# Order, input tile and last stores of the prepass in a gated mix of two attentions

## The chip, the core and the metric

One core of one Trainium2 chip runs the whole kernel. The metric is device time of one execution, in microseconds (us). The kernel before took 1770.2 us (median of 3 runs, 1770.02 to 1771.49).

## What is computed

The input x has 2048 tokens of 640 values, in bfloat16. The output is `g * a + (1 - g) * b`, with a gate g per token.

- `b` is local attention: 32 heads of width 20, where each token sees 8 tokens at distance 0, 2, ... 14 behind it.
- `a` is attention with a recurrent memory: 64 segments of 32 tokens, 32 heads of width 192. In front of a segment's 32 tokens stand 8 memory rows, which are the first 8 output rows of the segment before. So the segments run one after the other.

```python
for s in range(n_seg):                       # 64 segments
    h = jnp.concatenate([mem, xs], axis=1)   # 8 memory rows + 32 tokens
    q, k, v = (einsum('btd,dhe->bhte', h, W) for W in (Wq, Wk, Wv))
    scores = jnp.where(mask, einsum('bhqe,bhke->bhqk', q, k) * scale, -1e9)
    o = einsum('bhqk,bhke->bhqe', softmax(scores), v)
    o = einsum('bhte,hed->btd', o, Wo)
    mem = o[:, :8, :]                        # memory of the next segment
    outs.append(o[:, 8:, :])
x = A_x
out = sigmoid(x @ gate_w) * a + (1 - sigmoid(x @ gate_w)) * b
```

(This is the reference cut and slightly condensed.)

## The kernel before

**Part B** (`part_b`, L88 to L336; 0 to 232 us) computes `b` and the gate. x is transposed block by block, 512 tokens each (`make_xT`, L158), into a tile xT. From xT GpSimd (POOL) copies each block's tokens for the later segments (L184, L185, stored to DRAM), and the last 8 tokens of every segment into a tile zx (L190), which SyncE (SP) stores to a DRAM tensor zT_dram (L191). In the last quarter (L319 to L322) zT_dram is loaded back as tile zT, whose columns go by segment and token (s i), and POOL copies it into zTi, whose columns go by token and segment (i s). A step of part B is one block and one group of four heads. `proj` (L218), `scores` (L232) and `values` (L254) follow each other from step to step; DVE multiplies the exponentials by a band mask (L251).

**Prepass** (`prepass`, L419 to L477; 232 to 389.4 us). The last 8 tokens of each segment (positions 24 to 31) do not depend on the memory, so their Q, K and V for all 64 segments are computed at once, with 512 columns. `project_qk` (L426) does a pair of head groups: 24 groups of five matmuls of 128x512 (L438), each evacuated from PSUM into one tile ZS; ScalarE (ACT) and DVE take turns (L75, L77). When the pair is done two DMAs store ZS (L444), 8 segments first and then 56, in pieces of 192 values (384 B). `project_v` (L446) does one of four V rounds: four tiles ZV, 15 matmuls each (L453), and two stores of 192 KB per tile (L460). The order is pair 0, V 0, pair 1, V 1, pair 2, V 2, pair 3, V 3. Pairs read zT, V rounds read zTi. All results go into a DRAM tensor zpk_dram, one row of 1152 values per segment and partition: 384 of V, then 384 of K and 384 of Q.

**Part A** (`part_a`; 390 to about 1705 us) runs the 64 segments. A segment projects Q and K of the other 32 rows in eight groups (`m_qk`, L568; evacuated by `c_qk`, L577), transposes them (`t_qk`, L585), computes scores (`s_a`, L615 and `s_b`, L624), V (`m_v`, L661), the weighted sum (`pv_half`) and the output projection (`o_group`, L725). It loads the prepass's rows of the segment: `load_z` (L543) brings Q and K into part of the tile ZQ, and `load_vz` (L547) brings V. The scores need `load_z`; in the first segment all of these loads come right behind the prepass. For PE, ACT and DVE the order inside the loop is written out by hand; outside of it the order follows the program and the scheduler's priorities. The first segment's score matmul starts at 403.21 us. Part Z then multiplies the 8 last tokens of all segments by Wo in one go.

**Weights.** They are cut into 80 slices of 384 KB. 14 are streamed anew for each segment (tile wst, five buffers). 66 stay in SBUF and are loaded in four lots, as memory becomes free: "early" (21, during part B), "late 0" (24, when part B ends), "late 1" (8, asked for inside pair 3, L431) and "late 2" (13, after the prepass, L914). The lots are filled from a list that is sorted by first use (L371). All slice loads are issued by SP, in order.

**Queues.** SP and ACT issue the DMAs. Eight semaphores serve all of them in turn; a DMA waits until the transfer that used its semaphore before has landed. ACT also evacuates PSUM, in the same instruction order, so what stands behind a waiting DMA issue waits as well.

Of the kernel before, what the change touches and what calls it, by code (L numbers as in the profile page):

```python
# [10 lines left out]
BF = mybir.dt.bfloat16  # L11
# [4 lines left out]
N_EARLY = 21  # L16
N_MID = 8
ZVB = 4
N_LAST = 13
# [7 lines left out]
class _K:  # L27

    def __init__(self, ctx, tc, A_x, A_mem0, A_Wq, A_Wk, A_Wv, A_Wo, seg_len, B_wqkv, B_wo, gate_w, out):
# [22 lines left out]
        self.zctx = ExitStack()  # L52
# [35 lines left out]
    def part_b(self):  # L88
# [6 lines left out]
        self.zT_dram = self.dram.tile([128, KC, S // 32, 8], BF, name="zT_dram")  # L95
# [5 lines left out]
        with ExitStack() as ctx:  # L101
# [56 lines left out]
            def make_xT(b):  # L158
# [30 lines left out]
                zx = blkp.tile([128, KC, 16, 8], BF, name="zx_blk")  # L189
                nc.gpsimd.tensor_copy(zx[:].rearrange("p c s i -> p s c i"), xv[:, :, :, 24:32])  # L190
                nc.sync.dma_start(self.zT_dram[:, :, 16 * b:16 * b + 16, :].rearrange("p c s i -> p c (s i)"),  # L191
                                  zx[:].rearrange("p c s i -> p c (s i)"))
# [97 lines left out]
            zp = self.zctx.enter_context(tc.tile_pool(name="pre_z", bufs=1, side="right"))  # L290
            self.zT = zp.tile([128, KC, S // 4], BF, name="zT")
            self.zTi = zp.tile([128, KC, S // 4], BF, name="zTi")
            sel_ones = wp.tile([128, 160], BF, name="sel_ones")
            steps = [(b, g) for b in range((S + BQ - 1) // BQ) for g in range(8)]
# [7 lines left out]
            for i, (b, g) in enumerate(steps):  # L302
# [11 lines left out]
                if (b, g) == (1, 4):  # L314
                    self.build_sel(self.const, sel_ones[:])
# [3 lines left out]
                if (b, g) == (S // 512 - 1, 2):  # L319
                    nc.sync.dma_start(self.zT[:], self.zT_dram[:].rearrange("p c s i -> p c (s i)"))  # L320
                    nc.gpsimd.tensor_copy(self.zTi[:].rearrange("p c (i s) -> p c i s", i=8),
                                          self.zT[:].rearrange("p c (s i) -> p c i s", i=8))  # L322
# [33 lines left out]
    def weights_setup(self):  # L356
# [14 lines left out]
        use = [g for p in range(4) for g in (("qqkk"[p], 2 * (p % 2)), ("qqkk"[p], 2 * (p % 2) + 1), ("v", p))]  # L371
# [47 lines left out]
    def prepass(self):  # L419
# [6 lines left out]
        def project_qk(p, pool):  # L426
            m, Rp = "qqkk"[p], p % 2
            ZS = pool.tile([128, nseg, 192], BF, name="ZS")
            sls = [[self.get_slice((m, 2 * Rp + r, kc)) for kc in range(KC)] for r in range(2)]
            if p == 3:  # L430
                self.load_late(1)  # L431
            for r in range(2):
# [514 lines left out]
```

## Time and profile before

| What | us |
|---|---|
| median of the runs (3) | 1770.2 |
| the profiled execution's own time | 1772.28 |
| its span in the profile | 1770.6 |
| part B | 0 to 232.0 |
| prepass, first to last matmul | 232.03 to 389.39 |
| first segment ends | 428.43 |
| second segment ends | 448.87 |
| store of 56 segments of ZS, issue to landing, at 337.41 | 13.45 |
| one slice of 384 KB, alone | 3.1 to 3.2 |
| one slice more, while several load | 0.97 |

The profile comes from one execution. A row of a timeline gives start, duration, engine and line, tiles, count, and in brackets how long the engine was idle before it and what ended that. A row of "windows" gives the length of the stretch, the busy time of PE in it with the number of instructions that it is made of, the clock granted to the TensorE (1.00 is full), the busy share of the 16 DMA engines and what they moved. Rows of "DMA queue" give packets, MB, and the time that the packets took as a share of the 16 engines' time. "q10" is ACT's queue, "q1" SP's.

### The profile page before, as it was taken

Reading aid. Unit: us, or ns where it says so; the run is one execution under the profiler, and the core shown is the slowest. Engines: PE = TensorE matmul, PEld = TensorE weight load, DVE = VectorE, ACT = ScalarE, POOL = GpSimd, SP = SyncE. Lnnn points to the kernel's source line nnn. Section 1 sums busy time; section 2 is a strip of 40 time slices with the busy share of each in tenths; the row PEclk is TensorE's granted clock in tenths of the full one; section 3 lists DMA queues with packets and bytes.
Section 4 is the critical chain, followed back from the end, with each engine's and each line's share of the span. In section 5 each row is a group of like instructions: output and inputs, shape, how many; then the busy total and the mean of one; then the engine's idle time right before and its main releaser. Section 6 shows DMA issues by size and latency. Waiting matters only on the chain.

```text
span 1770.6 us, 82392 instructions
## 1 busy us (share of the span) xinstructions
PE 1675.4 (95%) x36512; PEld 995.8 (56%) x36527; DVE 651.8 (37%) x2047; ACT 869.2 (49%) x2377; POOL 75.0 (4%) x151
## 2 busy tenths in 40 slices
PE   6888999987999999999999999999999999999989
PEld 3555544434565655556555555555555555555557
DVE  4565532322333333333333333333333333333330
ACT  3766632223555555555555555555555555555550
POOL 6011000000000000000000000000000000000000
PEclk9999999998999999999999999999999999999999
DMA  5951176579999999899999989989989999998991
GB/s 161 331 128 50 38 258 164 154 234 328 290 303 303 303 301 306 297 297 311 302 298 303 306 284 304 302 289 297 304 297 298 301 298 303 303 296 292 306 299 30
DMA packets 283480, 467.81 MB, mean 264 GB/s; under 512 B 97524, under 2 KB 158452, under 8 KB 283124
## 3 DMA queue, kind: packets, MB, share of 16 engines
q1 hardware_dynamic: 181400, 403.14, 68.9%
q10 hardware_dynamic: 101724, 59.41, 11.6%
q8 instruction: 285, 4.67, 1.1%
q14 instruction: 71, 0.58, 0.1%
HBM read 428.13 MB, written 42.20 MB: 266 GB/s over the span
## 4 chain that ended last, share of the span: by engine, by line
PE 83%; ACT 6%; DMA 6%; issue 3%; DVE 1%; ACTq 0%; SPq 0%; POOL 0%; DVEq 0%; POOLq 0%
PE ps_qk L568 25%; PE ps_v L661 13%; PE ps_wo L725 11%; PE ps_qkT L585 6%; PE ps_S L615 5%; PE ps_pre L438 5%; PE ps_oT L684 3%; PE ps_z L879 3%; PE ps_bqk L224 3%; ACT bP L247 2%; PE ps_pre L453 2%; ACT ZQ L806 2%; PE ps_bv L211 1%; PE ps_mem L735 1%; PE ps_S L624 1%
## 5 line engine op out<-in xcount | busy, mean ns | idle before, releaser
L577 ACT CAST KV<-ps_qk 128x384 bf16<-128x384 f32 x448 | 208.5, 480 | 333.0 <-PE ps_qk L568 185.0
L568 PEld LDWEIGHTS <-hT 128*32 128x32 bf16 x10240 | 247.7, 96 | 154.5 <-DVE hT L738 12.8
L568 PE MATMUL ps_qk<-wlate_k,hT 128*32 128x384 bf16 x4352 | 269.9, 329 | 1.2 <-issue 0.9
L592 DVE COPY ZQ<-ps_qkT 128x384 bf16<-128x384 bf16 x256 | 91.6, 358 | 390.0 <-PE ps_qkT L585 220.3
L568 PE MATMUL ps_qk<-wres_q,hT 128*32 128x384 bf16 x4096 | 227.4, 329 | 4.6 <-ACT ZV L75 3.8
L633 ACT ACTIVATE ZQ<-ps_S 32x224 bf16<-32x224 f32 x512 | 178.1, 348 | 44.3 <-PE ps_S L624 39.8
L725 PEld LDWEIGHTS <-KV 128*32 128x32 bf16 x6144 | 154.1, 96 | 67.7 <-issue 20.2
L661 PE MATMUL ps_v<-wlate_v,hT 128*32 128x384 bf16 x2816 | 160.6, 329 | 0.0
L568 PE MATMUL ps_qk<-wst,hT 128*32 128x384 bf16 x1792 | 153.9, 329 | 1.0 <-issue 1.0
L661 PEld LDWEIGHTS <-hT 128*32 128x32 bf16 x5120 | 113.4, 96 | 72.7 <-issue 10.0
L725 PE MATMUL ps_wo<-wlate_oa,KV 128*32 128x384 bf16 x2560 | 140.5, 327 | 2.9 <-issue 2.8
L615 PE MATMUL ps_S<-ZQ,KV 128*128 128x160 bf16 (+1 forms) x1024 | 136.9, 238 | 3.3 <-DMA ZQ<-zpk_dram 3.3
L585 PE MATMUL ps_qkT<-ident,KV 128*128 128x128 bf16 x1536 | 130.7, 221 | 0.4 <-issue 0.3
L725 PE MATMUL ps_wo<-wlate_ob,KV 128*32 128x256 bf16 x2688 | 123.6, 275 | 7.3 <-issue 7.3
L585 PEld LDWEIGHTS <-KV 128*128 128x128 bf16 x1536 | 89.4, 98 | 61.9 <-issue 40.9
L695 DVE CAST KV<-ps_oT 128x192 bf16<-128x192 f32 x256 | 79.4, 351 | 64.8 <-PE ps_oT L689 64.8
L615 PEld LDWEIGHTS <-KV 128*128 128x128 bf16 (+1 forms) x1024 | 59.1, 95 | 72.6 <-issue 45.3
L695 ACT CAST KV<-ps_oT 128x192 bf16<-128x192 f32 x256 | 69.6, 326 | 59.0 <-PE ps_oT L689 59.0
L544 POOL COPY KTz<-ZQ 128x384 bf16<-128x384 bf16 x64 | 32.6, 509 | 1492.1 <-DMA ZQ<-zpk_dram 850.6
L661 PE MATMUL ps_v<-wst,hT 128*32 128x384 bf16 x1024 | 87.1, 330 | 9.1 <-DMA wst<-in_A_Wv_dram 9.1
L738 DVE CAST hT<-ps_mem 128x24 bf16<-128x24 f32 x126 | 22.6, 179 | 197.4 <-PE ps_mem L735 197.4
L668 ACT CAST KV<-ps_v 128x384 bf16<-128x384 f32 x192 | 92.4, 481 | 3.1
(127 smaller groups left out, 2316.8 us busy)
## 6 DMA issues: line engine op xcount, KB each, us to landing
wst<-in_A_Wq_dram SPq DMA_DIRECT2D x260, 384.0 KB
wst<-in_A_Wv_dram SPq DMA_DIRECT2D x260, 384.0 KB
wst<-in_A_Wk_dram SPq DMA_DIRECT2D x195, 384.0 KB
wst<-wscr SPq DMA_DIRECT2D x192, 384.0 KB
ZQ<-zpk_dram ACTq DMA_DIRECT2D x64, 192.0 KB
zpk_dram<-ZS ACTq DMA_DIRECT2D x4, 2688.0 KB
wscr<-in_A_Wo_dram SPq DMA_DIRECT2D x20, 384.0 KB
wlate_k<-in_A_Wk_dram SPq DMA_DIRECT2D x17, 384.0 KB
```

The lines of the kernel that those rows point to most:

```text
L224: nc.tensor.matmul(ps[:, 0:nn], lhsT=wqk[n][:, kc, 4 * g:4 * g + 4, :].rearrange("p h d -> p (h d)"), rhs=xT[:, kc, o0:o0 + nn], start=(kc ...
L438: nc.tensor.matmul(ps[:], lhsT=sls[r][kc][:, c0:c0 + 128], rhs=zT[:, kc, :], start=(kc == 0), stop=(kc == KC - 1))
L568: nc.tensor.matmul(pq[32 * j:32 * j + 32, 0:384], lhsT=hT[:, kc, :], rhs=sl[:, 384 * j:384 * j + 384], start=(kc == 0), stop=(kc == KC - 1 ...
L577: cp(sts[i], pqs[i][:, 0:384])
L585: nc.tensor.transpose(pT[:, t, :, :, :].rearrange("p j b i -> p (j b i)"), st[:, 128 * t:128 * t + 128], self.ident[:])
L592: nc.vector.tensor_copy(q_blocks(R)[:, 1:5, :, :].rearrange("p b c i -> p c b i"), pT.rearrange("p t j b i -> p (t j) b i"))
L615: nc.tensor.matmul(grid(h, par)[:, :, 0:80].rearrange("p j (b r i) -> p j b r i", r=2, i=8)[:, :, :, r, :], lhsT=KT[k0:k1, 12 * r + c:12 * ...
L633: nc.scalar.activation(E[ps], pSs[h][ps, :, 112 * j:112 * j + 112], ACT.Exp, scale=scale_a)
L661: nc.tensor.matmul(pvs[R][32 * j:32 * j + 32, 0:384], lhsT=hT[:, kc, :], rhs=sl[:, 384 * j:384 * j + 384], start=(kc == 0), stop=(kc == KC ...
L668: cp(V[R], pvs[R][:, 0:384])
L695: cps[j % 2](oTxs[2 * h + j // 2][:, 6 * (j % 2):6 * (j % 2) + 6, :], pos[j][:, 0:240].rearrange("p (c q) -> p c q", q=40)[:, :, 8:40])
L725: nc.tensor.matmul(pso[part][32 * jj:32 * jj + 32, 0:n], lhsT=oTxs[2 * (R // 2) + j // 2][:, 6 * (j % 2) + 3 * (R % 2) + t, :], rhs=o_weig ...
```

## The change

- V rounds come first, all four; then pairs 0, 1, 2, 3. All of them read zTi, in the order (i s). The evacuation of a pair reads PSUM as (i s) and writes (s i).
- zT, zT_dram, the store, the load and the POOL copy of zTi go. POOL copies the last tokens of each block straight into zTi (after the xh store). zTi is a tile TZ that lives for the whole kernel; in part A its bytes serve as K and V (KV), the K of the prepass (KTz) and a part ZA of what was ZQ. The rest of ZQ becomes ZB.
- Pair 3 is evacuated into two half tiles ZS0 and ZS1, each stored by itself in pieces of 96 values (192 B), 8192 pieces each. Pairs 0 to 2 have one store each instead of two.
- Early is 23 slices in place of 21, late 0 is 27 in place of 24, late 2 is 8 in place of 13. The list is sorted V, Q, K.
- The small memsets of V tiles (L206) go from POOL to DVE, and the masks (`build_sel`) are built at another point of part B.

```diff
-N_EARLY = 21
+N_EARLY = 23
-N_LAST = 13
+N_LAST = 8
...
+        self.TZ = self.const.tile([128, self.KC * self.S // 4], BF, name="TZ")
+        self.zTi = self.TZ[:].rearrange("p (c x) -> p c x", c=self.KC)
...
-                zx = blkp.tile([128, KC, 16, 8], BF, name="zx_blk")
-                nc.gpsimd.tensor_copy(zx[:].rearrange("p c s i -> p s c i"), xv[:, :, :, 24:32])
-                nc.sync.dma_start(self.zT_dram[:, :, 16 * b:16 * b + 16, :].rearrange("p c s i -> p c (s i)"),
-                                  zx[:].rearrange("p c s i -> p c (s i)"))
+                with tc.issue_after(xh_store.ins):
+                    nc.gpsimd.tensor_copy(zTi[:, :, :, 16 * b:16 * b + 16],
+                                          xv[:, :, :, 24:32].rearrange("p s c i -> p c i s"))
+                    if b == 3:
+                        self.build_sel(self.const, sel_ones[:])
...
-                    nc.gpsimd.memset(V[:, 640:652], 0.0)
+                    nc.vector.memset(V[:, 640:652], 0.0)
...
-                if (b, g) == (S // 512 - 1, 2):
-                    nc.sync.dma_start(self.zT[:], self.zT_dram[:].rearrange("p c s i -> p c (s i)"))
-                    nc.gpsimd.tensor_copy(self.zTi[:].rearrange("p c (i s) -> p c i s", i=8),
-                                          self.zT[:].rearrange("p c (s i) -> p c i s", i=8))
...
-        use = [g for p in range(4) for g in (("qqkk"[p], 2 * (p % 2)), ("qqkk"[p], 2 * (p % 2) + 1), ("v", p))]
+        use = [(m, R) for m in "vqk" for R in range(4)]
...
-            ZS = pool.tile([128, nseg, 192], BF, name="ZS")
+            if p < 3:
+                ZS = pool.tile([128, nseg, 192], BF, name="ZS")
...
             for r in range(2):
+                if p == 3:
+                    ZS = pool.tile([128, nseg, 96], BF, name=f"ZS{r}")
...
-                            nc.tensor.matmul(ps[:], lhsT=sls[r][kc][:, c0:c0 + 128], rhs=zT[:, kc, :],
+                            nc.tensor.matmul(ps[:], lhsT=sls[r][kc][:, c0:c0 + 128], rhs=zTi[:, kc, :],
...
-                        zc = 96 * r + 8 * (4 * t + j)
-                        self.evac(ZS[:, :, zc:zc + 8], ps[:].rearrange("p (s i) -> p s i", i=8))
-            z0 = 768 + 192 * (1 - Rp) if m == "q" else 384 + 192 * Rp
-            for s0, s1 in ((0, 8), (8, nseg)):
-                nc.scalar.dma_start(self.zpk_dram[s0:s1, :, z0:z0 + 192].rearrange("s p f -> p s f"), ZS[:, s0:s1, :])
+                        zc = 96 * r * (p < 3) + 8 * (4 * t + j)
+                        self.evac(ZS[:, :, zc:zc + 8], ps[:].rearrange("p (i s) -> p s i", i=8))
+                if p == 3 or r == 1:
+                    f0, f1 = (z0 + 96 * r, z0 + 96 * r + 96) if p == 3 else (z0, z0 + 192)
+                    nc.scalar.dma_start(self.zpk_dram[:, :, f0:f1].rearrange("s p f -> p s f"), ZS[:])
...
-        with tc.tile_pool(name="pre_zv", bufs=ZVB, side="right", reuse_waits="tile") as zvp, \
-                tc.tile_pool(name="pre_zs1", bufs=1, side="right", reuse_waits="tile") as zs1:
-            zT, zTi = self.zT, self.zTi
-            with tc.tile_pool(name="pre_zs0", bufs=1, reuse_waits="tile") as zs0:
-                project_qk(0, zs0)
-                project_v(0)
-                project_qk(1, zs1)
-                project_v(1)
-                project_qk(2, zs0)
-            project_v(2)
-            project_qk(3, zs1)
-            project_v(3)
-        self.zctx.close()
+        zTi = self.zTi
+        with tc.tile_pool(name="pre_zv", bufs=ZVB, side="right", reuse_waits="tile") as zvp:
+            for R in range(4):
+                project_v(R)
+        with tc.tile_pool(name="pre_zs0", bufs=1, reuse_waits="tile") as zs0:
+            project_qk(0, zs0)
+            with tc.tile_pool(name="pre_zs1", bufs=1, side="right", reuse_waits="tile") as zs1:
+                project_qk(1, zs1)
+            project_qk(2, zs0)
+        with tc.tile_pool(name="pre_zs2", bufs=1, side="right", reuse_waits="tile") as zs2:
+            project_qk(3, zs2)
...
-            ZQ = pers.tile([128, 224 + 768 + 1152], BF, name="ZQ")
+            ZB = pers.tile([128, 1536 + 160], BF, name="ZB")
+            KV, ZA = self.TZ[:, 0:1536], self.TZ[:, 1920:2528]
...
-                nc.scalar.dma_start(ZQ[:, 608:1376], self.zpk_dram[s, :, 384:1152])
+                nc.scalar.dma_start(ZB[:, 0:768], self.zpk_dram[s, :, 384:1152])
...
-    k.load_late(2)
+    k.load_late(2, "right")
```

More of the change, by code (lines that the diff above doesn't have):

```diff
@@ L51, in __init__ @@
         self.hTp = ctx.enter_context(tc.tile_pool(name="hTp", bufs=2))
-        self.zctx = ExitStack()
+        self.TZ = self.const.tile([128, self.KC * self.S // 4], BF, name="TZ")
+        self.zTi = self.TZ[:].rearrange("p (c x) -> p c x", c=self.KC)
         self._evac_i = 0
@@ L94, in part_b @@
         self.bsc_dram = self.dram.tile([S, 640], BF, name="bsc_dram")
-        self.zT_dram = self.dram.tile([128, KC, S // 32, 8], BF, name="zT_dram")
         self.oz_dram = self.dram.tile([S // 32, 128, 384], BF, name="oz_dram")
@@ L289, in part_b @@
             nc.scalar.preload_act_table_set("natural_log_exp_and_others")
-            zp = self.zctx.enter_context(tc.tile_pool(name="pre_z", bufs=1, side="right"))
-            self.zT = zp.tile([128, KC, S // 4], BF, name="zT")
-            self.zTi = zp.tile([128, KC, S // 4], BF, name="zTi")
+            steps = [(b, g) for b in range((S + BQ - 1) // BQ) for g in range(8)]
+            zTi = self.zTi.rearrange("p c (i s) -> p c i s", i=8)
             sel_ones = wp.tile([128, 160], BF, name="sel_ones")
-            steps = [(b, g) for b in range((S + BQ - 1) // BQ) for g in range(8)]
             self.first_store = None
@@ L314, in part_b @@
                 if (b, g) == (1, 4):
-                    self.build_sel(self.const, sel_ones[:])
                     self.hT0 = self.load_seg(0)
@@ L431, in project_qk @@
                 self.load_late(1)
+            z0 = 768 + 192 * (1 - Rp) if m == "q" else 384 + 192 * Rp
             for r in range(2):
+                if p == 3:
+                    ZS = pool.tile([128, nseg, 96], BF, name=f"ZS{r}")
                 for j in range(4):
@@ L523, in part_a @@
             pers = ctx.enter_context(tc.tile_pool(name="a_pers", bufs=1, reuse_waits="tile"))
-            ZQ = pers.tile([128, 224 + 768 + 1152], BF, name="ZQ")
-            Vz = ZQ[:, 224:608]
-            QTa = ZQ[:, 992:2144].rearrange("p (b r c i) -> p b r c i", b=6, r=2, i=8)
-            Es = [ZQ[:, 608 * h:608 * h + 224].rearrange("p (a f) -> p a f", a=2) for h in range(2)]
-            zst = ZQ[:, 32:416]
+            ZB = pers.tile([128, 1536 + 160], BF, name="ZB")
+            KV, ZA = self.TZ[:, 0:1536], self.TZ[:, 1920:2528]
+            Vz = ZA[:, 224:608]
+            QTa = ZB[:, 384:1536].rearrange("p (b r c i) -> p b r c i", b=6, r=2, i=8)
+            Es = [z[:, 0:224].rearrange("p (a f) -> p a f", a=2) for z in (ZA, ZB)]
+            zst = ZA[:, 32:416]
             oTz = zst.rearrange("p (c q) -> p c q", q=8)
-            whi = ZQ[:, 1376:1376 + 640]
-            KV = pers.tile([128, 1536], BF, name="KV")
+            whi = ZB[:, 768:768 + 640]
             KT = KV[:, 0:768].rearrange("p (c k) -> p c k", k=32)
@@ L534, in part_a @@
             oTxs = [v.rearrange("p (c q) -> p c q", q=32) for v in V]
-            a4 = pers.tile([128, 160], BF, name="a4")
-            KTz = pers.tile([128, 12, 32], BF, name="KTz")
+            a4 = ZB[:, 1536:1696]
+            KTz = self.TZ[:, 1536:1920].rearrange("p (c k) -> p c k", k=32)
             psm = ctx.enter_context(tc.tile_pool(name="psm", bufs=2, space=bass.MemoryType.PSUM, reuse_waits="tile"))
@@ L542, in load_z @@
             def load_z(s):
-                nc.scalar.dma_start(ZQ[:, 608:1376], self.zpk_dram[s, :, 384:1152])
+                nc.scalar.dma_start(ZB[:, 0:768], self.zpk_dram[s, :, 384:1152])
                 nc.gpsimd.tensor_copy(KTz[:].rearrange("p c (R i) -> p c R i", i=8),
-                                      ZQ[:, 608:992].rearrange("p (R c i) -> p c R i", c=12, i=8))
+                                      ZB[:, 0:384].rearrange("p (R c i) -> p c R i", c=12, i=8))
             def load_vz(s):
```

## The prediction

> **What bounds the kernel.** I read the page first, then the engines' busy time in windows around the end of the prepass, then the waits and the timelines there. All times are on the profiled execution's axis.
>
> ```profile
> span 1770.6 us, 82392 instructions
> PE 1675.4 (95%) x36512; PEld 995.8 (56%) x36527; DVE 651.8 (37%) x2047; ACT 869.2 (49%) x2377; POOL 75.0 (4%) x151
> ```
>
> TensorE is the bound, and what it computes does not change, so only its idle time can move. The windows show where that is (columns: length, PE busy with instructions, granted clock, DMA share, GB/s).
>
> ```profile
> 385.00:390.00 5.00, 4.34 (x20) 1.00 1.03 263
> 390.00:393.20 3.20, 0.01 (x4) 1.00 1.00 284
> 393.20:398.00 4.80, 4.37 (x62) 0.64 0.92 274
> 400.90:403.20 2.30, 0.00 (x0) 1.00 1.02 389
> 403.20:409.50 6.30, 6.29 (x94) 0.73 1.01 382
> 409.50:416.90 7.40, 0.04 (x4) 0.82 1.03 406
> 428.43:448.87 20.44, 20.20 (x509) 1.00 0.92 300
> ```
>
> The last prepass matmul ends at 389.39 (call this instant X) and the first of 64 segments at 428.43: 39.04 us, against 20.44 for the second segment, whose PE is busy 20.20. The loop from the second segment on keeps its instructions, order and waits; nothing is to be had there. So 18.6 us of transition are in play, and three waits make most of them:
>
> ```profile
> PE ps_v L661 <- DMA wst<-in_A_Wv_dram: 7.4, 1, 7.4
> PE ps_qk L568 <- ACT ZV L75: 4.1, 2, 3.8
> PE ps_S L615 <- DMA ZQ<-zpk_dram: 2.3, 1, 2.3
> ```
>
> The timelines of ScalarE's and SyncE's queues tell why:
>
> ```profile
> 382.82 9.63 ACTq L460 DMA_DIRECT2D zpk_dram<-ZV  x4
> 392.55 1.56 ACT L75 CAST ZV<-ps_pre 128x512 bf16<-128x512 f32 x3 [9.22 <-DMA wst<-in_A_Wk_dram]
> 396.60 0.73 ACTq L543 DMA_DIRECT2D ZQ<-zpk_dram  x1
> 397.45 6.71 SPq L399 DMA_DIRECT2D wlate_oa<-wscr  x6
> 404.20 4.40 SPq L399 DMA_DIRECT2D wlate_ob<-wscr  x7
> 409.13 3.26 SPq L401 DMA_DIRECT2D wst<-in_A_Wv_dram  x4
> ```
>
> ScalarE issues stores and evacuates, in order. A store whose semaphore (eight, used in turn) still belongs to a transfer in flight stands, and the evacuations behind it stand too: 9.22 us idle, and the loop's first matmuls start 3.80 late. Later the streamed V slice is queued behind 13 slices: the 7.4.
>
> **Part B.** Removed: the round trip and this POOL copy, which the DVE multiply beside it pays for:
>
> ```profile
> 142.13 4.83 POOL L321 COPY zTi<-zT 128x2560 bf16<-128x2560 bf16 x1 [9.89 <-DMA zT<-zT_dram]
> 144.30 3.76 DVE L251 TENSOR_TENSOR bP<-bP,band 128x968 bf16<-128x968 bf16 x2 [1.88 <-ACT bP L247]
> ```
>
> Two L251 take 1.46 elsewhere (728 ns mean), so 2.3 us of DVE, of which PE waited 1.26 at 149.15 (for DVE bo): −1.3. Added: the four 0.72-us copies (L190) become strided copies into TZ; by L321's 1.89 ns an element 1.21 each, and DVE may stand for it; and 20 small memsets go to DVE, which is idle over half of this stage (0.11 each on POOL). +0.6, between 0 and +2.3. build_sel is only moved, and two more early slices lengthen a load queue that ends long before the prepass. **Part B −0.7**, between −1.3 and +1.
>
> **Prepass.** 720 matmuls at 0.2159 us are 155.4; it took 157.36 (232.03 to 389.39), of which 1.9 are waits. Reading PSUM as (i s) and writing strided costs nothing: both engines' evacuations of a pair (ACT 593, DVE 692 ns) lie under 2.16 us of matmul; without that cover each ns longer would count 72 times. V first gives 32 ZV stores while late slices still load (before: 231.37 to 257.2); stores and loads then wait for each other's semaphores. With a ZV store at 3 to 4 us and eight semaphores ScalarE falls little behind eight PSUM banks: I take **−0.9**, half the waits gone, between −1.9 and +4 (a stand of 9.22 us less five spare banks at 1.08 us of matmul each).
>
> **The transition.** Price of a packet first. Two windows in which one queue moves almost alone:
>
> ```profile
> q10 hardware_dynamic: 5474, 2.10, 99.3%
> q1 hardware_dynamic: 2370, 0.70, 96.8%
> ```
>
> The first (339 to 347, ZS store) is 384-B packets: 0.993 x 16 x 8 us / 5474 = 23.2 ns on an engine. The second (103 to 106) is 320- and 256-B packets, mean 295 B: 19.6 ns. The line through them gives 15.5 at 192 B; I take 16. Bounds: 23.2 (no cheaper than 384 B) and 7.6 (bytes alone, at a 3072-B packet's 121 ns). A half tile is 8192 packets, 512 on each engine: 8.2 us by 16 ns, and about 2 to land. The whole store takes 13.45 today (issued 337.41), so two halves cost 16.4 us of DMA where one full store costs 11.9.
>
> Order in the built program: SyncE issues late1's eight slices when p=2's store has landed, about X−11.5 (X−25.9, +0.6 evacuation, +13.9). ScalarE issues half 0 at X−11.2 (X−12.95, +1.7). They share the engines: 8.2 + 2 + eight slices at 0.97 (7.8) + three streamed slices (2.6) = 20.6, half 0 lands at **X+9.4**. Behind the last evacuation ScalarE has, in order: the Vz load, which takes half 0's semaphore and so stands until X+9.4; half 1's store (X+10); two c_qk; load_z, which needs half 1 landed; c_qk(3). So:
> - X+1.0: PE enters the loop; the 3.8-us gap shrinks to 1.0.
> - X+3.5: PE wants c_qk(0)'s bank and stands to X+10.4 (6.9).
> - Half 1: 8.2 + 2 + four slices of late2 released by half 0 (3.9): lands X+23.8. PE stands again for c_qk(3) and the scores.
> - load_z: 4.6 more with late2's next slices beside it (today 6.57; in the loop 4.8 to 7.3): first score matmul at X+28.4. Today X+13.8.
> - From the first scores a steady segment needs 14.5 (434.35 to 448.87), plus 1.7 for half clock after the wait, as at 403: end **X+44.6**. The streamed V slice, behind eight slices instead of 13, lands near X+32.7; wanted at X+34.7. The 7.4 goes.
>
> 44.6 − 39.04 = **+5.6**. What is late next after the V slice is half 1 and load_z. Each ns of packet price moves two times 0.512 us: at 23.2 ns +13.0, at 7.6 −3.0.
>
> [...]
>
> **Sum:** −0.7 − 0.9 + 5.6 = **+4.0**. The profiled execution took 1772.28 (span 1770.6) and would take 1776.3; the median of the runs shown is 1770.2, so 1774.2. 0.2% (3.5 us) is about what a measurement of this kernel can tell from no change.
>
> **Rivals.**
> 1. *The stores do land early.* If half 0 lands by X+1.4 (late1 loads behind it, not beside it), all that follows is 8 us earlier; what is left is the shorter last queue: X+36.6, −2.4; with −1.6 total −4.0, **1766.2**. It decides at X+5.4: half 0 landing sooner than that makes the kernel faster. For it: a 192-KB ZV store lands in 3 us when alone. Against: the queues alternate, and 9.6 us of slices are released within 1.5 us of half 0.
> 2. *Halves cost as much as wholes*: 23.2 ns a packet, total +11.4, **1781.6**. For it: 320 and 256 B are already only 15% under 384. [...]
> 3. *The V rounds stall* on semaphores, +4 in place of −0.9: total +8.9, **1779.1**. For it: the 9.22 row. Against: no ZS store lies ahead of V now.
> 4. *It cancels*: half 0 at X+5.4; late1 gives way by half, **1770.2**. The edit then merely moves the wait from L661 to L615.
>
> **Chances.** Forecast 0.45 (of which 0.15 ends under +3.5); rival 1 0.22, rival 2 0.15, rival 3 0.08, rival 4 0.10. Faster by over 0.2%: 0.22 (rival 1; its −4.0 is past −3.5). Within: 0.15 + 0.10 = 0.25. Slower: 0.30 + 0.15 + 0.08 = 0.53. The range goes from rival 1 with part B and prepass at their low ends (−2.4 − 1.3 − 1.9 = −5.6, 1764.6) to rival 2 (1781.6); it leaves out cheap packets under rival 1 and dear ones with stalls, under 2 in 10.
>
> **What would show it.** Right: ScalarE's Vz load issue standing 8 us after X; c_qk(0) after it; a 6-us PE gap before the third projection, a longer one before L615's first scores, none at L661; half stores landing 14 to 21 us after issue, their packets at 16 ns; first segment ending 44 to 45 us after X; no 3.2-us L251. Wrong: half 0 landed before X+5, PE idle over 2 us in the V rounds, or a segment after the first that differs from 20.4 us.

## The result and the profile after

The changed kernel took 1781.07 us (median of 4 runs, 1779.57 to 1784.05) against 1770.11 us for the kernel before (4 runs, 1769.2 to 1771.49): ratio 1.0063 [1.0046, 1.0081]. Measured again with more runs, the same pair gave 1772.88 (12 runs) against 1765.3 (35 runs): 1.0035 [1.0015, 1.0054]. So it is slower, by 6 to 11 us. The profiled execution took 1779.57.

The page of the changed kernel, the two lines that answer those of before:

```profile
span 1777.4 us, 82403 instructions
PE 1672.4 (94%) x36527; PEld 997.5 (56%) x36527; DVE 651.0 (37%) x2065; ACT 869.2 (49%) x2377; POOL 71.3 (4%) x132
```

PE is busy 3 us less and the span is 6.8 us longer: idle time was added. X, the end of the last prepass matmul, is 384.29 here. The windows behind it (length, PE busy, PEld, DVE, ACT, POOL, granted clock, DMA share, GB/s; the share adds up the times of packets and can pass 1):

```profile
384.29:386.84 2.55, 2.55 (x60) 1.44 (x60) 0.69 (x1) 0.00 (x0) 0.00 (x0) 1.00 1.57 170
386.84:396.41 9.57, 0.00 (x0) 0.00 (x0) 0.00 (x0) 0.53 (x2) 0.00 (x0) 0.74 0.85 181
396.41:401.05 4.64, 4.63 (x49) 2.13 (x49) 0.72 (x2) 0.81 (x2) 0.00 (x0) 0.50 0.95 314
401.05:410.12 9.07, 0.00 (x1) 0.00 (x1) 0.36 (x1) 0.53 (x2) 0.00 (x0) 0.50 0.85 195
412.96:429.85 16.89, 16.12 (x360) 9.21 (x360) 5.30 (x20) 8.11 (x26) 0.51 (x1) 0.83 0.89 293
429.85:449.60 19.75, 19.59 (x494) 12.06 (x494) 7.30 (x27) 10.59 (x32) 0.51 (x1) 1.00 0.94 309
```

PE enters the loop at once, where before it came 3.8 us late, and then stands twice, 9.57 and 9.07 us; behind the first the granted clock is 0.50, behind the second 0.50 (410.12 to 412.96) and then 0.83. The waits of PE in the first segment name who released it:

```profile
PE ps_qkT L581 <- ACT TZ L573: 18.6, 2, 9.6
PE ps_S L611 <- DMA ZB<-zpk_dram: 2.3, 1, 2.3
```

The wait for the streamed V slice (7.4 before) is gone, the one for load_z is as long as it was, and 18.6 us for ScalarE's evacuation of Q and K is new. ScalarE's timeline shows why it is late:

```profile
383.25 0.58 ACT L76 CAST ZS<-ps_pre 128x512 bf16<-128x512 f32 x1 [1.57 <-PE ps_pre L436]
394.97 0.35 ACTq L544 DMA_DIRECT2D TZ<-zpk_dram  x1
395.44 0.40 ACTq L442 DMA_DIRECT2D zpk_dram<-ZS  x1
395.88 0.86 ACT L573 CAST TZ<-ps_qk 128x384 bf16<-128x384 f32 x2 [12.05 <-issue]
409.15 0.34 ACTq L539 DMA_DIRECT2D ZB<-zpk_dram  x1
409.59 0.86 ACT L573 CAST TZ<-ps_qk 128x384 bf16<-128x384 f32 x2 [12.10 <-DMA zpk_dram<-ZS]
```

Between 383.83 and 394.97 it does nothing: the Vz load (L544, issued at 394.97) has the semaphore of half 0's store (L442, issued at 371.60) and stands until that lands, at X+10.6. Then half 1 goes out, two evacuations follow, and load_z (L539) stands until half 1 has landed, at X+24.8. What the stages add to the span:

| stage | before | after | difference | forecast |
|---|---|---|---|---|
| part B | 232.03 | 225.90 | −6.1 | −0.7 |
| prepass | 157.36 | 158.39 | +1.0 | −0.9 |
| X to the end of the first segment | 39.04 | 46.07 | +7.0 | +5.6 |
| segments 2 to 63 | 1259.9 | 1263.9 | +4.0 | 0 |
| the rest (segment 64 and behind it) | | | +0.9 | 0 |
| span | 1770.6 | 1777.4 | +6.8 | +4.0 |

### The profile page after: what moved, and what is told of

Same layout as the page of the kernel before. It is cut to its first block, busy times and chain, and to the rows that moved or that the text cites. A ratio compares the mean times of both kernels' runs of the same rounds, so it can differ in the third digit from the quotient of the medians.

```text
span 1777.4 us, 82403 instructions
## 1 busy us (share of the span) xinstructions
PE 1672.4 (94%) x36527; PEld 997.5 (56%) x36527; DVE 651.0 (37%) x2065; ACT 869.2 (49%) x2377; POOL 71.3 (4%) x132
## 4 chain that ended last, share of the span: by engine, by line
PE 84%; ACT 6%; DMA 5%; issue 3%; DVE 2%; ACTq 0%; DVEq 0%
PE ps_qk L564 25%; PE ps_v L657 13%; PE ps_wo L721 11%; PE ps_qkT L581 6%; PE ps_pre L436 5%; PE ps_S L611 5%; PE ps_oT L680 3%; PE ps_z L875 3%; PE ps_pre L451 3%; PE ps_bqk L225 3%; ACT bP L248 3%; DMA zpk_dram<-ZS 2%; ACT ZB L802 2%; PE ps_mem L731 1%; PE ps_S L620 1%
## 5 line engine op out<-in xcount | busy, mean ns | idle before, releaser
L573 ACT CAST TZ<-ps_qk 128x384 bf16<-128x384 f32 x448 | 208.1, 479 | 356.5 <-PE ps_qk L564 185.3
L657 PE MATMUL ps_v<-wres_v,hT 128*32 128x384 bf16 x4096 | 224.0, 328 | 0.0
L721 PEld LDWEIGHTS <-TZ 128*32 128x32 bf16 x6144 | 153.8, 96 | 72.7 <-issue 24.3
L581 PE MATMUL ps_qkT<-ident,TZ 128*128 128x128 bf16 x1536 | 131.0, 222 | 18.6 <-ACT TZ L573 18.6
L721 PE MATMUL ps_wo<-wlate_oa,TZ 128*32 128x384 bf16 x2560 | 140.2, 327 | 3.4 <-issue 3.4
L611 PE MATMUL ps_S<-ZB,TZ 128*128 128x160 bf16 (+1 forms) x1024 | 137.2, 238 | 3.1 <-DMA ZB<-zpk_dram 2.9
L721 PE MATMUL ps_wo<-wlate_ob,TZ 128*32 128x256 bf16 x2688 | 124.2, 275 | 8.5 <-issue 8.4
L564 PE MATMUL ps_qk<-wlate_q,hT 128*32 128x384 bf16 x2304 | 130.0, 329 | 1.3 <-issue 1.1
L564 PE MATMUL ps_qk<-wres_q,hT 128*32 128x384 bf16 x1792 | 109.2, 329 | 0.2
L629 ACT ACTIVATE ZB<-ps_S 32x224 bf16<-32x224 f32 x256 | 89.0, 348 | 41.4 <-PE ps_S L620 38.3
L611 PEld LDWEIGHTS <-TZ 128*128 128x128 bf16 (+1 forms) x1024 | 59.0, 95 | 71.8 <-issue 44.6
L734 DVE CAST hT<-ps_mem 128x24 bf16<-128x24 f32 x126 | 22.5, 179 | 201.3 <-PE ps_mem L731 201.3
L664 ACT CAST TZ<-ps_v 128x384 bf16<-128x384 f32 x192 | 92.3, 481 | 3.2
```

Source lines behind the costliest of these rows:

```text
L564: nc.tensor.matmul(pq[32 * j:32 * j + 32, 0:384], lhsT=hT[:, kc, :], rhs=sl[:, 384 * j:384 * j + 384], start=(kc == 0), stop=(kc == KC - 1 ...
L573: cp(sts[i], pqs[i][:, 0:384])
L581: nc.tensor.transpose(pT[:, t, :, :, :].rearrange("p j b i -> p (j b i)"), st[:, 128 * t:128 * t + 128], self.ident[:])
L611: nc.tensor.matmul(grid(h, par)[:, :, 0:80].rearrange("p j (b r i) -> p j b r i", r=2, i=8)[:, :, :, r, :], lhsT=KT[k0:k1, 12 * r + c:12 * ...
L629: nc.scalar.activation(E[ps], pSs[h][ps, :, 112 * j:112 * j + 112], ACT.Exp, scale=scale_a)
L657: nc.tensor.matmul(pvs[R][32 * j:32 * j + 32, 0:384], lhsT=hT[:, kc, :], rhs=sl[:, 384 * j:384 * j + 384], start=(kc == 0), stop=(kc == KC ...
```

## The experiments

The stage that the forecast priced came out nearly as priced; two others, that it had near nothing for, moved by 6.1 and 4.0 us with opposite signs. Two questions follow: are those two the change's doing, and what sets the length of the transition? For the second there are three theories. **T1**, the prediction's: ScalarE issues and evacuates in order, so a store that lands late holds everything behind it. **T2**: the 192-B packets are dear, for a reason of size or address. **T3**: from X to the end of the first segment the DMA engines are full, and the length is the transfer work that is left at X; the order of the queues only chooses which instruction waits.

To compare runs I use one mark: the start of the first matmul that picks the memory rows, 0.5 us ahead of the first segment's end. It is at X+38.54 before and X+45.56 after; the loop in the table is counted between such marks.

### The two kernels once more

Nothing is changed in either.

> The changed kernel again, unedited, for a second profile. Theory 1 (the extra time sits in the transition; the loop's +4.4 us in the first pair of profiles is chance in how late instruction fetches come): transition from the last prepass matmul to the first segment's end again 46 us, but the mean of the later segments back at 20.3 us, and a median near 1776. Rival (the loop itself became slower by the change): mean segment again 20.40 us or more, median again near 1781. Part B: if its -6.1 us came from half-clock stretches that happened to miss this run, it will differ by 2 to 5 us this time; if it came from the copies, it stays at 225.9 us.

> The kernel before once more, for a second profile. Theory 1 (part B and the loop vary from run to run by several us for reasons that have nothing to do with the change): part B differs from 232.0 by more than 1 us, or the mean segment from 20.32; the prepass (157.4) and the transition (first segment's end at +39.0) stay within 1 us. Rival (part B of the kernel before is always near 232 and the copies were worth 4 to 6 us): 232 again.

Kernel after: ratio 1.0035 [1.0015, 1.0054], the first scores at X+29.5, the mark at X+45.90, prepass 158.39 again, part B 228.5, loop 1257.6. Kernel before (a single run): 1766.61 us, mark X+40.60, part B 226.49 in place of 232.03, loop 1253.5 in place of 1259.9. So the transition repeats to 0.3 us in the changed kernel and to 2.1 in the one before (its V slice came later, a wait of 8.6 in place of 7.4), while part B and the loop move by 5.5 and 6.4 us between two executions of the *same* kernel. Part B moves with the clock. One window of it in the kernel before, in the first profile:

```profile
205.00:220.00 15.00, 14.44 (x220) 9.51 (x220) 7.60 (x21) 9.67 (x27) 0.00 (x0) 0.77 0.07 24
```

and in the changed kernel:

```profile
205.00:220.00 15.00, 14.79 (x237) 10.68 (x239) 7.47 (x25) 8.35 (x27) 0.00 (x0) 1.00 0.10 36
```

A granted clock of 0.77 for 15 us against 1.00; the second profile of before has 1.00 there as well, and all versions of the changed kernel end part B anywhere from 225.9 to 231.1. The loop's waits, changed kernel, 450 to 1690 us:

```profile
PE ps_wo L721 <- issue: 14.6, 22, 1.3
PE ps_oT L680 <- issue: 4.6, 8, 0.9
```

In a version with the same loop (pad_64 below):

```profile
PE ps_wo L721 <- issue: 6.4, 11, 1.5
PE ps_oT L680 <- issue: 4.0, 8, 1.1
```

"issue" means that PE waited for nothing that the profile shows. Added up, these waits go from 16.5 to 27.0 us in the 14 profiles of this study, and the loop from 1251.6 to 1263.9; the correlation is 0.94, with 1.1 us of loop for 1 us of wait. The two profiles of before have 23.5 and 21.0, the changed kernel 26.0 and 22.8. So the loop's +4.0 lies within what one kernel does by itself.

### ScalarE without the stand: vz_from_sync

The first Vz load goes to SP's queue, so that ScalarE no longer waits for half 0.

```diff
-            load_vz(0)
+            nc.sync.dma_start(Vz, self.zpk_dram[0, :, 0:384])
```

> The first segment's Vz load is issued by SyncE, so that on ScalarE nothing stands ahead of the second half's store. Theory 1 (ScalarE stands on the semaphore of the first half, and this is what delays the second half): the second half's store is issued about 1 us after the last prepass matmul instead of 11, c_qk follows at once, the 9.6-us gap of PE goes, the second half lands at about +17 instead of +24.8, the first scores come near +21 instead of +28.7; 6 to 8 us faster than the changed kernel. Rival (the engines are full anyway, so that an earlier issue only shares them): second half lands at +22 or later, and the gain is under 3 us.

Ratio 1.0027 [1.001, 1.0045]; first scores X+26.3, mark X+43.13: 2.4 us earlier only. The waits:

```profile
PE ps_qkT L581 <- ACT TZ L573: 16.3, 2, 12.7
PE ps_S L611 <- DMA ZB<-zpk_dram: 2.3, 1, 2.3
```

Half 1 is issued at X+0.8 in place of X+11.15, yet lands at X+22.5 in place of X+24.8: it takes 21.7 us, because it now runs beside the other half. So the first stand of ScalarE, which T1 blames, is worth 2.4 of the 7.0 us by itself.

### The address of the halves: row_1280 and pad_64

A row of zpk_dram is 2304 B long and half 0 starts 1152 B into it. row_1280 makes every row a multiple of 512 B and leaves the offsets. pad_64 has the same row length and shifts K and Q by 64 values (128 B).

```diff
-        self.zpk_dram = self.dram.tile([nseg, 128, 1152], BF, name="zpk_dram")
+        self.zpk_dram = self.dram.tile([nseg, 128, 1280], BF, name="zpk_dram")
...
-            z0 = 768 + 192 * (1 - Rp) if m == "q" else 384 + 192 * Rp
+            z0 = 832 + 192 * (1 - Rp) if m == "q" else 448 + 192 * Rp
...
-                nc.scalar.dma_start(ZB[:, 0:768], self.zpk_dram[s, :, 384:1152])
+                nc.scalar.dma_start(ZB[:, 0:768], self.zpk_dram[s, :, 448:1216])
```

(The first edit is row_1280; all three are pad_64.)

> The rows of zpk_dram are 1280 values instead of 1152, so that every row begins on a multiple of 512 B and the first half's 192 B (offset 1152) no longer cross such a line in every second row; they still cross a 256-B line. Theory 1 (a piece that crosses a 512-B line costs twice): the first half runs at 262 GB/s like the second instead of 146, 12.6 ns a piece instead of 21; it lands 4 to 5 us earlier, at about +6, and so does all that follows: 4 to 5 us faster than the changed kernel. The whole store of pair 1 (at 1536, crossing none) lands in under 12 us, pairs 0 and 2 stay at 13.7. Rival (256-B lines matter, or the row pitch, or which half it is): first half stays at 146 GB/s, no gain.

> Rows of zpk_dram of 1280 values, and K and Q begin 64 values later: the first half's 192 B now lie within one 256-B line (1280 to 1472), the second half's cross one (1472 to 1664). Theory 2 (a piece that crosses a 256-B line is dear, 512-B lines having been ruled out): the roles change; the first half runs at 262 GB/s, the second at 146 where it is alone, and the first half lands 4 to 5 us earlier than in the changed kernel (+6), the second one as much later after its issue. Rival (it is not the place in DRAM, but the tile ZS0 or the order): first half again at 146 GB/s, landing at +10.6.

row_1280: ratio 1.0029 [1.001, 1.0048], half 0 lands at X+10.1, mark X+43.96; nothing of the 512-B row shows in the packets (half 0 moves at 149 GB/s from 387 to 390, in the changed kernel at 146 from 386.4 to 388.4). pad_64 is the telling one, though its mark (X+46.32) is that of the changed kernel and its time (1769.54, a single run, against 1767.35) settles nothing: the two halves trade places. Half 0 lands at X+7.6 (X+10.6 without the shift), half 1 takes 17.8 us (13.7). The DMA view of the changed kernel while half 0 is nearly alone, 386.4 to 388.4:

```profile
DMA packets 1487, 0.29 MB, mean 146 GB/s; under 512 B 1485, under 2 KB 1485, under 8 KB 1487
```

and half 1 of the same kernel, 403 to 407:

```profile
DMA packets 5129, 1.05 MB, mean 263 GB/s; under 512 B 5105, under 2 KB 5105, under 8 KB 5129
```

In pad_64, half 1, 404.4 to 407.4:

```profile
DMA packets 2271, 0.44 MB, mean 145 GB/s; under 512 B 2271, under 2 KB 2271, under 8 KB 2271
```

2 us on 16 engines for 1487 packets is 21.5 ns each, and 4 us for 5129 is 12.5; with the shift half 1 pays 3 us for 2271, 21.1. Half 0's pieces reach from byte 1152 to 1344 of a row and cross a 256-B boundary (1280), half 1's from 1344 to 1536 do not; with the shift it is the other way round, and so are the prices. A crossing costs about 8.8 ns a packet, 4.5 us for a half store. T2 is right in this form, not in the 512-B form.

The two prices are some 70% apart. Pieces of 384 B show what goes with the price. Pair 0's begin 128 B behind a boundary and pair 2's on one, and both cost 23.5 ns (5452 and 5442 packets in 8 us, 306 to 314 and 362 to 370 in the changed kernel). In all these cases it is how many 256-B lines a piece touches: 21 to 24 ns for two, 12.5 for one.

### Half 0 ahead of the slices: late1_last

Rival 1 asked for a half 0 that lands by X+1.4, late1 loading behind it. Here late1's eight slices move to the lot that is asked for after the prepass.

```diff
-N_MID = 8
+N_MID = 0
...
-N_LAST = 8
+N_LAST = 16
```

> No slices are loaded beside the last pair (N_MID 0), all 16 come after the prepass (N_LAST 16). Theory 1 (eight slices beside the first half delay it): the first half lands about 10 us earlier, near +1 or before, ScalarE does not stand, the second half is issued near +1.5 and lands near +17 beside slices; the first scores near +22; then the streamed V slice, behind 16 slices, is late by several us as in the kernel before. Sum about 1773 to 1777. Rival (the first half is slow by itself, at 21 ns a piece 10.8 us): it lands at about 0 all the same, so the two differ in the stand of ScalarE only if slices matter; should it land later than +5 with no slices beside it, theory 1 is wrong.

Ratio 1.0041 [1.0023, 1.0059]. Half 0 landed at X+1.38, as rival 1 has it (and took 14.07 us with nothing beside it, as long as a whole pair's store); the first scores came at X+20.9, 7.7 us earlier. But the mark is at X+45.37, not 8 us earlier:

```profile
PE ps_qkT L581 <- ACT TZ L573: 13.0, 1, 13.0
PE ps_v L657 <- DMA wst<-in_A_Wv_dram: 7.2, 1, 7.2
```

The V slice is late again, behind 16 slices. Rival 1 got its condition and lost its gain, though not quite in its own form: here late1's eight slices lengthen the last queue, which rival 1 has short. It fits T3: the same transfers, in another order, the same end.

### The last pair in one tile: whole_last, split_segments

whole_last stores the last pair like the others, in 384-B pieces. split_segments does that too, but in two stores, 8 segments and then 56, as the kernel before did.

```diff
-            if p < 3:
+            if True:
...
-                if p == 3 or r == 1:
-                    f0, f1 = (z0 + 96 * r, z0 + 96 * r + 96) if p == 3 else (z0, z0 + 192)
-                    nc.scalar.dma_start(self.zpk_dram[:, :, f0:f1].rearrange("s p f -> p s f"), ZS[:])
+            for s0, s1 in ((0, 8), (8, nseg)) if p == 3 else ((0, nseg),):
+                nc.scalar.dma_start(self.zpk_dram[s0:s1, :, z0:z0 + 192].rearrange("s p f -> p s f"), ZS[:, s0:s1, :])
```

(This is split_segments; whole_last has one store of all segments there.)

> The last pair in one whole tile again, one store; all else of the change stays. Theory 1 (halves cost a stand, since a half takes the engines about as long as a whole, and the first one meets eight slices): nothing stands ahead of the store, issued near +1.2 after the last prepass matmul, alone on the engines; lands at +15, first scores near +19 (changed kernel +28.7), streamed V slice late by 1 to 2 us, first segment's end near +37 to +38 instead of +46: 7 to 9 us faster than the changed kernel, 1 to 3 faster than the kernel before. Rival (halves bring the store forward by 13 us of matmul, so without them the scores come later): scores after +28, slower than the changed kernel.

> Last pair in one tile, stored as in the kernel before: 8 segments first, then 56. The first segment's load then needs only the short store. Theory 1: short store issued near +1.2, landed near +5, first scores near +10; the wait then moves to the streamed V slice, which stands behind late 2, and late 2 behind the long store (lands near +16): V slice near +27, first segment's end near +38, no gain over the whole store. Rival (late 2 does not matter with 8 slices): end near +27.

whole_last: ratio 1.0003 [0.9981, 1.0025], mark X+41.30, that is 4.3 us earlier than with halves. Its one store lands at X+17.75, the waits are 13.8 (ScalarE), 3.5 (V slice) and 1.1 (load_z). split_segments: ratio 1.0019 [1.0002, 1.0036], mark X+41.37; the early short store gained nothing at the end. It landed at X+6.11 and load_z went out at X+6.13, but load_z took 10.69 us: it is on ScalarE's own queue behind the long store, which landed at X+16.45. Most of that, 7.98 us, is the issue itself, in which ScalarE does nothing else:

```profile
393.05 7.98 ACTq L536 DMA_DIRECT2D ZB<-zpk_dram  x1
```

### Two more orders: split_z_sync, late2_after_v

split_z_sync is split_segments with the first load_z on SP's queue. late2_after_v is that, and the last eight slices are asked for only behind the first segment's V slices.

```diff
-                nc.scalar.dma_start(ZB[:, 0:768], self.zpk_dram[s, :, 384:1152])
+                (nc.scalar if s else nc.sync).dma_start(ZB[:, 0:768], self.zpk_dram[s, :, 384:1152])
...
-            self.nc.sync.dma_start(v[:], src)
+            self.last_load = self.nc.sync.dma_start(v[:], src).ins
...
+                if s == 0:
+                    with tc.issue_after(self.last_load):
+                        self.load_late(2, "right")
...
-    k.load_late(2, "right")
```

(The first edit is split_z_sync; all of them are late2_after_v.)

> As split_segments, but the first segment's load of K and Q is issued by SyncE, so that it isn't behind the long store in ScalarE's queue. Theory 1 (in split_segments that load took 10.7 us because it lay in one queue with the long store): it now lands in 4 to 6 us, first scores near +11 instead of +18.9; the streamed V slice then is what is late, since late 2 stands ahead of it until the long store has landed (+16.5): a stall of 9 us or more at the V matmuls, first segment's end again near +41, no gain in sum. Rival (the engines, not the queue, made it slow): scores after +16.

> As split_z_sync, and late 2 is issued behind the first segment's four V slices. Theory 1 (the order of the last queue is what is left): scores near +11, no stall at V, then one of some 4 to 7 us at the output projection, whose streamed slice is behind late 2; first segment's end near +31 to +33, 13 us before the changed kernel and 6 to 8 before the kernel before: ratio to before 0.996. Rival (the stall only moves, to the output projection, whole): end after +38, ratio 1.000 or more.

split_z_sync: ratio 1.0021 [0.9996, 1.0047], first scores at X+11.74 (28.68 in the changed kernel, 13.82 before), mark X+42.14. Its waits:

```profile
PE ps_v L654 <- DMA wst<-in_A_Wv_dram: 12.9, 1, 12.9
PE ps_S L608 <- DMA ZB<-zpk_dram: 6.5, 1, 6.5
```

late2_after_v: ratio 0.9998 [0.9971, 1.0025], mark X+39.56:

```profile
PE ps_wo L718 <- DMA wst<-wscr: 10.1, 1, 10.1
PE ps_S L608 <- DMA ZB<-zpk_dram: 6.5, 1, 6.5
```

Scores 17 us earlier made the end 3 to 6 us earlier. The wait walks from Q and K (18.6) to the V slice (12.9) and on to the output projection's slice (10.1); each kernel cures the last one's symptom. That is T3's picture. One order was not run: all of these issue the long store of segments 8 to 63 within 2 us of X, and none holds it back until the first segment has what it needs. The last eight slices would have to wait with it, since they wait for that store here (SyncE's wait in late2_after_v: `SPq L393 <- DMA zpk_dram<-ZS: 5.8, 1, 5.8`).

### Less left at X: v_last, v_last_left

If T3 holds, it takes less transfer work behind X to shorten the transition. v_last runs the pairs first and the V rounds last (as the kernel before ends), all pairs whole, with the list sorted Q, K, V. The K and Q stores have landed 45 us before X; what is left at X are V's small stores and the eight slices.

```diff
-        use = [(m, R) for m in "vqk" for R in range(4)]
+        use = [(m, R) for m in "qkv" for R in range(4)]
...
-        with tc.tile_pool(name="pre_zv", bufs=ZVB, side="right", reuse_waits="tile") as zvp:
-            for R in range(4):
-                project_v(R)
...
         with tc.tile_pool(name="pre_zs2", bufs=1, side="right", reuse_waits="tile") as zs2:
             project_qk(3, zs2)
+        with tc.tile_pool(name="pre_zv", bufs=ZVB, side="right", reuse_waits="tile") as zvp:
+            for R in range(4):
+                project_v(R)
```

v_last_left only takes `side="right"` away from the pool pre_zv.

> The changed kernel with the last pair whole and the order turned: four pairs first, then the four V rounds; the slices' list is sorted Q, K, V. All else of the change stays (one x^T, shared bytes, 8 slices at the end). Theory 3 (what sets the first segment's end is the DMA work that is left behind the last prepass matmul: 42 us of engine time in the changed kernel, 37 in the one before, 38 with a whole tile, however it is ordered): here the stores of K and Q lie under V's matmuls, and behind the end there are only the last V stores, 8 slices and the segment's own; load_z is issued before the end, scores near +5, V slice late by 0 to 3 us, DMA work behind the end under 27 us, first segment's end at +20 to +25: 13 to 18 us faster than the kernel before, ratio 0.990 to 0.993. Rival (V stores and slices collide at the end as in the kernel before, whose V rounds were last too): ScalarE stands behind a store as there, first segment's end at +33 or later, ratio 0.996 or more.

> As v_last (pairs first, V rounds last, last pair whole), but the ring of ZV tiles lies on the other side of the memory, where only its second tile overlaps the last pair's ZS. Theory (the 6.83-us wait at the start of the V rounds in v_last is that tile waiting for the store of ZS, and the transition is set by the transfers behind X): the waiting evacuation comes 14 matmuls, 3.0 us, later, so the wait shrinks to 3 to 4 us; prepass 163 instead of 166.8; first segment's end stays at X+26 to X+29; span 3 to 4 us under that of v_last at an equal mean segment; ratio 0.995 to 0.998. Rival (the wait is for weights of V, or for semaphores): the prepass stays at 166 to 167 and the ratio at 0.999. A second rival, that the first segment's early end was a matter of one execution: it ends at X+38 or later.

The stretch from X to the first segment's end, in windows: the kernel before,

```profile
389.39:428.43 39.04, 24.87 (x488) 14.22 (x487) 7.86 (x27) 11.79 (x34) 0.51 (x1) 0.83 0.95 323
```

the changed kernel,

```profile
384.29:430.36 46.07, 24.32 (x489) 13.49 (x489) 7.61 (x26) 10.31 (x31) 0.51 (x1) 0.70 0.92 245
```

and v_last, to its mark:

```profile
393.90:420.82 26.92, 20.85 (x473) 12.44 (x473) 7.72 (x26) 10.53 (x32) 0.00 (x0) 0.94 0.96 333
```

The DMA share is 0.92 to 0.96 in all three, and the length is what differs: 39, 46, 27. But the share is an average. It passes 1 while small packets move, whose times overlap (1.57 from 384.29 to 386.84), and so it hides stretches in which the engines have next to nothing to move. The changed kernel has two (length, PE busy, granted clock, DMA share, GB/s):

```profile
393.00:396.40 3.40, 0.00 (x0) 0.50 0.14 21
407.20:410.60 3.40, 0.48 (x3) 0.50 0.22 26
```

Each lies at the end of a half store. Half 0's packets are nearly all through by X+8.7 and the last one by X+9.6; the landing is told at X+10.6; only then are the Vz load, half 1 and the next of late 2's slices issued, and the engines are full again from X+12.1. The kernel before has no such hole; its emptiest stretch, under which PE works, is this:

```profile
420.50:425.50 5.00, 4.99 (x174) 0.94 0.66 188
```

So I split the time from X to the mark in two, counting no quarter of a microsecond as more than full (an estimate from the packets' records, one profile each):

| kernel | X to mark | DMA share | engines empty | engines moving |
|---|---|---|---|---|
| before | 38.5 | 0.95 | 2.9 | 35.6 |
| before_again | 40.6 | 0.92 | 4.3 | 36.3 |
| after | 45.6 | 0.92 | 8.6 | 37.0 |
| same_again | 45.9 | 0.91 | 9.3 | 36.6 |
| vz_from_sync | 43.1 | 0.98 | 5.1 | 38.0 |
| row_1280 | 44.0 | 0.94 | 7.5 | 36.5 |
| pad_64 | 46.3 | 0.93 | 8.8 | 37.5 |
| late1_last | 45.4 | 0.91 | 6.2 | 39.2 |
| whole_last | 41.3 | 0.92 | 6.4 | 34.9 |
| split_segments | 41.4 | 0.94 | 5.6 | 35.8 |
| split_z_sync | 42.1 | 0.90 | 6.9 | 35.2 |
| late2_after_v | 39.6 | 0.95 | 4.9 | 34.7 |
| v_last | 26.9 | 0.96 | 1.5 | 25.4 |
| v_last_left | 28.2 | 0.93 | 2.7 | 25.5 |

(The 42, 37 and 38 us of the expectation of v_last are length times share, which counts the overlap twice.) Half of T3 stands: the time that the engines move is about 35 to 39 us in every kernel but the two of v_last's order, which leave less at X and have 25. The program sets it, not the length: SyncE's queue moves 2654 to 2702 packets of 3072 B up to the mark in every kernel with eight late slices, in 27 us or in 46, against 3301 and 3310 in the kernel before and 3689 in late1_last. The other half of T3, that the engines are full, is wrong for the changed kernel. Its engines move for about 1 us longer than those of the kernel before, with fewer bytes (245 x 46.07 against 323 x 39.04: 11.3 and 12.6 MB), and are empty for about 5 us longer, which is most of its longer transition. vz_from_sync, in which half 1 is queued before half 0 has landed, has only the second hole left (2.5 us at a share of 0.15), and whole_last has one of 3.5 us (0.12). So T1's chain, a landing that everything behind it waits for, is where the change lost most of its time, and T3's work is a floor that no order but v_last's took below 34.7 us.

v_last takes 11.6 us out of the transition and is still no faster: ratio 0.999 [0.9968, 1.0011]; v_last_left 0.9996 [0.9977, 1.0015]. The prepass gives it back. PE's waits in v_last's prepass:

```profile
PE ps_pre L449 <- ACT ZV L76: 6.8, 1, 6.8
PE ps_pre L434 <- DVE ZS L78: 2.3, 3, 0.8
```

ScalarE's wait behind the first is `ACT ZV L76 <- DMA zpk_dram<-ZS`, 15.3 us: the first ZV tile lies where the last pair's ZS lay, whose store of 13.9 us must land first. Prepass 166.8 in place of 158.4. In v_last_left only the second ZV tile lies there, and the first tile's evacuations get through. ScalarE's stand fell from 15.3 to 11.1 us, which bears out that the memory is what it waits for, but PE still stood 5.64 us where 3 to 4 were expected, the clock was 0.54 in the 6 us behind it, and the prepass took 167.1: no gain. A version whose ZV ring lies nowhere on that ZS was not run, so what v_last gives without the wait stays open; an estimate is its 1.8 us (0.999 of 1768.35) and the 6.8 of the wait, 8 to 9 us under the kernel before.

## Why the prediction was right, and where it was not

**The sum.** Forecast +4.0, measured +7.3 by the profiled executions (1779.57 against 1772.28) and +11.0 by the medians of the first measurement, inside its range by half a microsecond, and slower as forecast. The sum came that near partly by luck: part B was 5.4 us lower than forecast and the loop 4.0 higher, and both are no more than two executions of one kernel differ by. What the change itself does is the transition (+7.0, or +5.0 against the second profile of before), the prepass (+1.0) and part B's removed wait (−1.4, below): +4.6 to +6.6. The longer comparison's ratio, 1.0035 of 1765.3, is +6.2 [+2.6, +9.5].

**The transition: right, with errors that nearly cancel.** Half 0 was forecast at X+9.4 and landed at X+10.6, though issued 1.5 us earlier than forecast (X−12.7): it took 23.3 us in place of 20.6, more than the 14 to 21 that were named as a sign of being right (late1's slices and half 0 shared the engines, 545 packets of SyncE's queue and 547 of ScalarE's from 379 to 383); half 1 was to be issued at X+10 and land at X+23.8, and did at X+11.15 and X+24.8; the first scores were forecast at X+28.4 and came at X+28.7; the V slice's wait of 7.4 went, as said; the segment was to end at X+44.6 and ended at X+46.1. The first wait was not c_qk(0)'s bank at X+3.5 but one step earlier, the transposes that read it, at X+2.55, and so 9.6 us in place of 6.9; the segment's end depends on the second wait and did not see this. Half 1 took 13.7 (13.8 forecast), with cheaper packets, and load_z with what follows 3.8 (4.6). The missing 1.5 us: 1.2 for half 0, the rest probably the clock, 0.50 from 396 to 413 and 0.83 in the stretch behind.

**The packet price: right in sum, wrong in form.** One price of 16 ns was taken for both halves. Measured are 21.3 and 12.5, mean 16.9. That the two errors cancel is luck. Rival 2's 23.2 is nearly true for half 0 alone.

**What sets it: the right chain, but not alone.** The prediction followed one chain (ScalarE behind a semaphore), and the runs bear it out: the two holes at the halves' landings are most of the loss. Taking away the first stand (vz_from_sync) closed one hole and gave back 2.4 of the 7.0 us, because half 1 then shared the engines. Of the 7.0 us, 4.3 are the halves (whole_last), and the other 2.8 (0.7 against the second profile of before) the order: with V first, a pair's store stands last, of 11.9 us of packets, where V's two stores stood. Five slices less in the last lot (4.85 us at 0.97) had been counted as the gain for V's slice; they were used up by this. What did not hold is rival 1's "all that follows is 8 us earlier": late1_last met its condition, X+1.38, and ended at X+45.4 by the mark, with eight more slices in its last queue.

**The prepass: small and wrong.** The forecast had half of the 1.9 us of waits go and feared a stall in the V rounds (rival 3). There was no stall. But one wait of 0.78 us came in each of the last three pairs:

```profile
319.65 0.59 PE L436 MATMUL ps_pre<-TZ,wlate_q 128*128 128x512 bf16 x2 [0.78 <-DVE ZS L78]
```

The group needs the PSUM bank that DVE is just emptying (318.91, 0.69 us). "Both engines' evacuations lie under 2.16 us of matmul" counts the engines' time, not which bank comes next. It is 2.3 us in sum, for the 1.2 that went. ("72 times" counts the V rounds too, whose evacuation is not changed; it is 48 an engine for the pairs, and nothing hangs on it.)

**Part B: right in its term.** The two multiplies that paid for POOL's copy (3.76 us) are short again:

```profile
141.98 0.67 DVE L252 TENSOR_TENSOR bP<-bP,band 128x968 bf16<-128x968 bf16 x1 [1.88 <-ACT bP L248]
142.85 0.67 DVE L252 TENSOR_TENSOR bP<-bP,band 128x968 bf16<-128x968 bf16 x1 [0.20 <-ACT bP L248]
```

and the wait of 1.26 behind them is gone: from the next Q projection to the scores it is 2.17 us (144.39 to 146.56), where it was 3.58 (146.71 to 150.29). That is a gain of 1.4, forecast 1.3. The strided copies take 1.26 us each, forecast 1.21, and 18 memsets went to DVE, not 20. The other 4.7 us are mostly the clock (0.77 in the window shown).

**The loop: right, but it was not known why.** "Nothing to be had there" holds of the change; that a profile's loop varies by 12 us over 14 executions could not be seen in one, and makes a single span a poor judge of 4 us. For the same reason the sign "a segment after the first that differs from 20.4 us" was no use: the second took 19.75 by the marks, and segments take 19.7 to 22.0 in both kernels.

## What to carry to other kernels

Behind a stage that leaves transfers open, add up the transfer time left, by packet price and not by bytes, and compare it with the compute that is to hide it: if the engines are full, reordering queues moves the wait and not the end (here the engines moved for 34.7 to 39.2 us in every order but v_last's). Look also for holes, in which all that is queued waits for one landing: an average share hides them, and each landing that the next stage waits for opened one of 2.5 to 3.5 us here. A piece of a store that crossed a 256-B boundary cost nearly as much here as one twice its size (192 B: 21.1 to 21.5 ns; 384 B: 23.2 to 23.5; 192 B within one line: 12.5), so cut at such boundaries or not at all. And before a difference in a profile is put down to a change, see how much that stage moves between two executions of one kernel.

## What had not been expected of the hardware

- A 192-B packet took 21.1 to 21.5 ns across a 256-B boundary and 12.5 ns within one; a 384-B packet took 23.2 to 23.5 ns, and always touches two lines here. The length of the row (2304 or 2560 B) made no difference.
- A load issued on ScalarE's queue behind a long store took 10.69 us (split_segments), 7.98 of them in the issue, and 5.65 us on SP's queue at the same time (split_z_sync).
- Stretches of half clock in part B, with PE over 90% busy (0.77 over the 15 us shown), came and went between executions of one kernel, whose part B ended 5.5 us apart.
- The waits called "issue" in the loop seem to be instruction fetches. In the changed kernel, 1000 to 1040 us, the DMA queues list 7 packets of 16 KB in a queue of instructions:

```profile
q8 instruction: 7, 0.11, 1.1%
```

PE's timeline in that stretch has this gap, and one such packet starts 1.7 us ahead of it, on engines that the weights keep 0.9 busy:

```profile
1014.61 0.19 PE L685 MATMUL ps_oT<-ZB,TZ 32*128 32x32 bf16 x2 [0.78 <-issue]
```

From 450 to 1690 us there are 234 such packets, 5.3 us apart in the mean, and 35 "issue" waits of PE over 0.3 us. Each of the 35 begins 1.1 to 2.5 us behind the start of a packet, where chance would spread them over 5 us. This is inferred from the times; no run took the fetches away. Of the 234 packets, 199 are followed by no such wait. If the inference holds, the fetches cost the 16.5 to 27.0 us a run that these waits add up to.
